# Sliding-window attention: dense key blocks on TensorE in place of shifted products on VectorE

## The chip, the core and the metric

The kernel runs on one core of a Trainium2 chip. The core has a matrix engine (TensorE, PE in the profile, with its weight loads as PEld), a vector engine (VectorE, DVE), an engine for pointwise functions (ScalarE, ACT), GpSimd (POOL) and a sync engine whose queue (SPq) issues transfers. PE reads its operands from SBUF and writes to PSUM, eight banks of 512 fp32 columns on 128 partitions. The metric is the device time of one execution in microseconds (us); lower is better.

## The reference

Four layers on a sequence of 2048 rows of 512 features, in the order A, B, A, B. Each adds to `x` a function of its layer norm. A is a long convolution whose kernel comes from a state-space model, done by Fourier transforms. B is what changes here:

```python
H = 32; Dh = D // H                     # 32 heads of 16 features
W, dil = 8, 2
qkv = (x @ wqkv) ...                    # (3, H, S, Dh)
idx = pos[:, None] - (jnp.arange(W) * dil)[None, :]
mask = idx >= 0
logits = jnp.einsum("bhsd,bhswd->bhsw", q, kg) * Dh ** -0.5
logits = jnp.where(mask, logits, -1e9)
attn = softmax(logits, axis=-1)
o = jnp.einsum("bhsw,bhswd->bhsd", attn, vg)
return o @ wo
```

So a query at position s looks at eight keys: s, s-2, s-4, to s-14. Even positions see only even ones, and odd ones only odd ones.

## The kernel before

The sequence stands in SBUF as `X[p, j, :]`, position 16 p + j, with 128 partitions p and 16 slots j. `kernel_and_first_conv` computes the convolution's kernel and the first A layer (0 to 268 us), `b_layer` the first attention layer (268 to 402), `a_layer` the second A layer (402 to 468), and `b_layer` again the second attention layer (468 to 602), with the store of the result.

An attention layer goes like this. `start(q)` norms four slots on DVE, transposes them on PE into `pt_x` and copies them to `xnT`, half of them by ACT (L807) and half by DVE (L805), so that features stand on partitions and positions in columns, ordered j first. `proj_qk` (L815) makes queries and keys with four matmuls of 512 columns a tile, copied out by ACT (L824). For each of the eight offsets w, `qk_products` (L845) multiplies queries with shifted keys on DVE (L855, and L863 where the shift crosses a partition), and PE sums groups of 16 features with the small matrix `bones` into `Lp` (L868). The logits are transposed back (L876), and `softmax` (L880) takes maximum, exponential (ACT, L902), sum, reciprocal and product on whole tiles. `proj_v` (L828) makes the values, and two transfers put a copy `Vp`, one partition lower, beside `V`. `pv` (L916) multiplies values with weights on DVE for each offset (L924), and PE adds the eight products by matmuls with the identity, which transpose them as well (L939); ACT copies the sum to `oT` (L942). `out` (L944) multiplies by `wo`, adds `X` by an identity matmul (L950) and copies back to `X` (L951). In the first attention layer it also gathers the statistics of the next norm.

`load_b_weights` (L116) loads the weights over SP's queue, with a permutation of `wo` in the transfer and one of the value weights on ACT (L831). `Conv.final` (L295) and `final` in `a_layer` (L744) write the convolution's result back to `X`, eight or four neighbouring slots at a time. `s1` in `a_layer` (L685) does the first stage of the transform, four slots at a time. `a_layer` holds four spectra `Kt` of 1 MB, loaded from DRAM.

The order within an engine comes from the framework's planner: it places instructions by priority, which is the order of the program, as soon as their inputs and a free buffer are there by its own costs. `at(tc, marks[q])` gives a part the priority of an earlier place in the program; `room` reserves such a place. Semaphores are added by the framework. Engines take their instructions in the order planned.

## Time and profile before

| | us |
|---|---|
| median of three runs | 604.02 |
| lowest and highest run | 603.73, 607.95 |
| span of the profiled execution | 606.0 |
| its two attention layers | 134, 134 |

The span is from the first to the last instruction of one profiled execution; the runs are device times of other executions, and the median stands 2.0 us under the span. The page gives busy time by engine, the span in 40 slices, the chain of work that ended last and the costliest groups of instructions. A row of a group reads: line, engine, operation, written tile <- read tiles, partitions x elements, count | busy us, mean ns of one | idle time just before them and what ended it. A row in order of time reads: start, us from start to end of the run of instructions, engine, line, operation, count. A matmul's duration contains its latency; in a run, the next one starts long before it is over.

### The profile page before, as it was taken

What the parts mean: (1) busy time and instruction counts of PE and PEld (TensorE: products, weight loads), DVE (VectorE), ACT (ScalarE), POOL (GpSimd) and SP (SyncE); (2) the same over time, 40 slices, a digit from 0 to 9 for tenths busy, and PEclk for the clock granted to TensorE, in tenths of its full rate; (3) what the DMA queues carried; (4) which work ended last, traced back from release to release, by engine and by line L of the source; (5) the groups of instructions that cost most, each with busy time, mean ns of one, the idle gap of its engine ahead of it and who ended that gap; (6) DMA issues with size and microseconds to landing.
All of it is one profiled execution on the core that took longest, in us unless ns stands there. A gap on an engine that the chain in (4) does not pass through costs nothing.

```text
span 606.0 us, 12631 instructions
## 1 busy us (share of the span) xinstructions
PE 422.6 (70%) x5362; PEld 261.7 (43%) x5402; DVE 497.0 (82%) x942; ACT 323.0 (53%) x449; POOL 12.9 (2%) x50
## 2 busy tenths in 40 slices
PE   1102565865775575559998678977996899857996
PEld 0101343562462463245333466644764433326762
DVE  5999999799899996366877899965999688689950
ACT  4999355455465343526576213466984556722144
POOL 0000000000000002100000000000000000000000
PEclk9999787696797797758999599997998899978999
DMA  8101354624735627510001333005530000040011
GB/s 293 62 1 35 61 104 66 140 55 106 121 98 99 103 91 136 129 70 1 1 1 39 83 137 143 2 1 125 85 71 0 2 1 1 1 121 1 1 71 69
DMA packets 75093, 41.31 MB, mean 68 GB/s; under 512 B 65825, under 2 KB 70818, under 8 KB 73758
## 3 DMA queue, kind: packets, MB, share of 16 engines
q1 hardware_dynamic: 73454, 40.12, 27.2%
q8 instruction: 42, 0.69, 0.5%
q10 hardware_dynamic: 1584, 0.39, 0.3%
q14 instruction: 13, 0.11, 0.1%
HBM read 15.89 MB, written 8.39 MB: 40 GB/s over the span
## 4 chain that ended last, share of the span: by engine, by line
PE 27%; DVE 21%; ACT 9%; issue 7%; DMA 2%; POOL 0%; SPq 0%; POOLq 0%; ACTq 0%
PE ps_qk L822 7%; DVE prod L924 6%; PE ps_o L948 4%; PE ps_v L836 3%; PE Lp L868 2%; PE pt_x L802 2%; PE po L939 2%; DVE prod L863 1%; DVE ln_st_b L152 1%; ACT xc L711 1%; DVE pa L719 1%; DMA zt<-Z 1%; DVE pb L720 1%; ACT oT L942 1%; PE ps_o L950 1%
## 5 line engine op out<-in xcount | busy, mean ns | idle before, releaser
L939 PE MATMUL po<-sb_ident,prod 128*128 128x128 bf16 x1024 | 70.4, 227 | 13.7 <-DVE prod L924 10.3
L939 PEld LDWEIGHTS <-prod 128*128 128x128 bf16 x1024 | 62.3, 102 | 23.5 <-DVE prod L924 20.1
L822 PE MATMUL ps_qk<-xnT,wqk 128*128 128x512 bf16 x245 | 63.7, 391 | 4.3 <-ACT xnT L807 2.3
L855 DVE TENSOR_TENSOR prod<-qT,kT 128x2048 bf16<-128x2048 bf16 (+3 forms) x48 | 43.2, 953 | 14.0 <-ACT qT L824 7.2
L924 DVE TENSOR_TENSOR prod<-V,L 128x2048 bf16<-128x2048 bf16 (+3 forms) x48 | 43.8, 955 | 6.4 <-PE po L939 6.4
L942 ACT CAST oT<-po 128x1024 bf16<-128x1024 f32 x16 | 15.4, 1015 | 56.6 <-PE po L939 56.6
L863 DVE TENSOR_TENSOR prod<-qT,kT 128x2048 bf16<-128x2048 bf16 (+3 forms) x40 | 35.0, 903 | 6.9 <-ACT kT L824 4.3
L204 PE MATMUL psA<-X,sb_F 128*128 128x128 bf16 x128 | 13.7, 237 | 34.5 <-ACT X L575 33.7
L822 PEld LDWEIGHTS <-wqk 128*128 128x128 bf16 x256 | 23.4, 100 | 32.1 <-issue 11.8
L948 PE MATMUL ps_o<-wo_t,oT 128*128 128x512 bf16 x121 | 33.5, 380 | 4.9 <-ACT oT L942 3.9
L204 PEld LDWEIGHTS <-sb_F 128*128 128x128 bf16 x256 | 17.4, 106 | 42.6 <-issue 40.0
L924 DVE TENSOR_TENSOR prod<-Vp,L 128x2048 bf16<-128x2048 bf16 (+3 forms) x40 | 35.0, 903 | 0.0
L532 PE MATMUL psk<-Ytab,Xtab 128*32 128x64 bf16 x1024 | 23.7, 206 | 12.9 <-DVE Ytab L513 5.6
L191 ACT CAST Z<-psA 128x1024 bf16<-128x1024 f32 (+1 forms) x32 | 28.6, 979 | 7.3 <-PE psA L204 7.3
L535 PE MATMUL psk<-Y2tab,Xtab 128*32 128x48 bf16 x1024 | 22.8, 202 | 13.5 <-issue 12.2
L868 PE MATMUL Lp<-prod,sb_bones 128*32 128x512 bf16 x256 | 24.9, 410 | 10.1 <-DVE prod L863 5.1
L513 DVE TENSOR_TENSOR Ytab<-Ytab,MA 128x2048 bf16<-128x2048 bf16 (+1 forms) x33 | 30.7, 931 | 0.2
L152 DVE BATCH_NORM_STATS2 ln_st_b<-X 128x6 f32<-128x384 bf16 (+2 forms) x80 | 23.7, 358 | 8.6 <-ACT X L309 8.6
L515 DVE TENSOR_TENSOR Y2tab<-Ytab,MB 128x2048 bf16<-128x2048 bf16 (+1 forms) x33 | 30.7, 930 | 0.0
L836 PE MATMUL ps_v<-wv,xnT 128*128 128x512 bf16 x126 | 28.2, 379 | 1.8 <-ACT V L838 1.7
L532 PEld LDWEIGHTS <-Xtab 128*32 128x32 bf16 x1024 | 20.9, 105 | 17.8 <-issue 15.5
L222 PE MATMUL psA<-zt,sb_C 128*128 128x512 bf16 x30 | 15.6, 548 | 18.6 <-DMA zt<-Z 14.4
(184 smaller groups left out, 1022.3 us busy)
## 6 DMA issues: line engine op xcount, KB each, us to landing
kt_scratch<-Kt SPq DMA_DIRECT2D x4, 1024.0 KB, 3.9
Kt<-kt_scratch SPq DMA_DIRECT2D x4, 1024.0 KB, 6.8
Vp<-V SPq DMA_DIRECT2D x2, 1568.0 KB, 9.1
X<-in_A_u_dram SPq DMA_DIRECT2D x4, 512.0 KB, 5.1
Xr<-in_A_u_dram SPq DMA_DIRECT2D x4, 512.0 KB, 5.1
out_dram<-X SPq DMA_DIRECT2D x4, 512.0 KB, 2.6
k_scratch<-KTq SPq DMA_DIRECT2D x7, 256.0 KB, 2.0
KT<-k_scratch SPq DMA_DIRECT2D x7, 256.0 KB, 2.8
```

The costliest lines, as they stand in the source:

```text
L204: nc.tensor.matmul(o, F1[:, j, r, :], rhs_j(j), start=True, stop=not dk)
L513: nc.vector.tensor_tensor(v(Y[:, :, :, q * EYB:(q + 1) * EYB, :]), src, vm(self.mult(self.MA, lev, hc, EYB)), ALU.mult)
L515: nc.vector.tensor_tensor(v(Y2[:, :, :, (q - 1) * EYB:q * EYB, :]), src, vm(self.mult(self.MB, lev, hc, EYB)), ALU.mult)
L532: nc.tensor.matmul(psk[32 * g:32 * g + 32, ds, :], xs, Y[:, m // 2, h, :, t], start=(m == 0), stop=False, skip_group_check=True)
L822: nc.tensor.matmul(ps[:], wqk[:, ct, f0:f0 + 128], xnT[:, ct, s0:s0 + 512], start=(ct == 0), stop=(ct == 3))
L836: nc.tensor.matmul(ps[:].rearrange("p a b -> p (a b)"), xnT[:, ct, j * 128:(j + 1) * 128], wv[:, ct, :], start=(ct == 0), stop=(ct == 3))
L855: nc.vector.tensor_tensor(pr[:, :, (ja - j0) * 128:(ja - j0) * 128 + n], qT[fp][:, :, ja * 128: ja * 128 + n], kT[fp][:, :, (ja - sh) * 12 ...
L863: nc.vector.tensor_tensor(pr[:, :, 0:n], qT[fp][:, :, q0: q0 + n], kT[fp][:, :, k0: k0 + n], ALU.mult)
L868: nc.tensor.matmul(Lp[r0:r0 + 32, w // 4, :], bones[:, w % 4, :], pr[:, f2, hb * 512:(hb + 1) * 512], start=(w % 4 == 0), stop=(w % 4 == 3 ...
L924: nc.vector.tensor_tensor(p2[:, ja - j0: ja - j0 + n, :].rearrange("p j (t d h) -> p (j t) d h", t=2, d=DH), src.rearrange("p j (t d h) -> ...
L939: nc.tensor.matmul(po[f2][:, jj, :], p2[:, jj, f2 * 128:(f2 + 1) * 128], ident[:], start=(w == 0 and jj % 4 == 0), stop=(w == W - 1), skip ...
L948: nc.tensor.matmul(ps[:], oT[:, ft, j * 128:(j + 1) * 128], wo_t[:, ft, :], start=(ft == 0), stop=False)
```

## The change

The eight shifted products are replaced by dense matmuls. Positions are split by parity, and each parity's 1024 positions into 9 blocks of 114 queries, which need the 7 keys before the first one: 121 keys, held in a block of 128. For each of 4 quarters `n` (parity by half of the heads) and 9 blocks `b`, `logits` multiplies a head's keys by its queries, 128 by 114, as 16 matmuls for 16 heads. A head has 16 features, but its matmul contracts over 32 rows: the other 16 hold constants (`_mask_rows`), whose product adds a large negative number wherever the key lies outside the window of eight. Two heads share 32 partitions, one in the even and one in the odd rows; `KS` and `QS` hold both arrangements, and the constants are loaded once. ACT takes the exponential straight from PSUM, without subtracting a maximum. `values` uses the exponentials as the stationary operand and a head's 16 values, with a column of ones, as the moving one of 17 columns: the last column is the sum. DVE takes its reciprocal and scales; PE transposes the result back, two matmuls a block, and DVE copies three blocks at a time to `oT`.

Queries and keys reach `KS` and `QS` by transfers, because the features have to be spread over every second partition: ACT and DVE copy a projection to `st`, and SP issues two transfers for each pair of projections, 32 of 128 KB a layer. The quarter `n + 1` is projected during quarter `n`, in two sets of buffers. The 8 output projections of the even positions are placed in the last quarter, the others behind it.

So that four slots of one parity can go together, slots are taken in the order given by `slot` in the norms' statistics, in `final`, in `s1`, and in the store. The copies in `Conv.final` are now of four slots each. `a_layer` keeps two spectra `Kt` at a time. The weights and the constants are loaded over GpSimd's queue, and ACT permutes the query and key weights once. The diff, cut to its core:

```diff
+def slot(m):
+
+    g, i = m // 4, m % 4
+    return 8 * (g % 2) + 2 * i + g // 2
...
-def load_b_weights(nc, const, C, wqkv, wo):
...
+def load_b_weights(nc, const, tmp, C, wqkv, wo):
     wqk = const.tile([128, 4, 1024], BF, name="wqk")
     wv = const.tile([128, 4, 512], BF, name="wv")
     wo_t = const.tile([128, 4, 512], BF, name="wo_t")
-    wvn = const.tile([128, 4, 512], BF, name="wvn")
     wsrc = wqkv.rearrange("(t p) f -> p t f", p=128)
-    nc.sync.dma_start(wqk[:], wsrc[:, :, 0:1024])
-    nc.sync.dma_start(wvn[:], wsrc[:, :, 1024:1536])
-    for ft in range(4):
-        src = wo[ft * 128:(ft + 1) * 128, :].rearrange("(h d) o -> d h o", d=DH)
-        nc.sync.dma_start(wo_t[:, ft, :], src)
-    nc.sync.dma_start(C["bones"][:], nc.inline_tensor(_bf(bones_np), name="c_bones").ap())
-    Vp = const.tile([128, 2, NJ - 2, 256], BF, name="Vp")
-    nc.gpsimd.memset(Vp[0:1], 0.0)
-    return dict(wqk=wqk, wv=wv, wvn=wvn, wo=wo_t), Vp
+    eng = nc.gpsimd
+    wq_in = tmp.tile([128, 4, 1024], BF, name="wq_in")
+    eng.dma_start(wq_in[:], wsrc[:, :, 0:1024])
+    for w in range(2):
+        for e in range(2):
+            nc.scalar.copy(wqk[:, :, w * 512:w * 512 + 512].rearrange("p t (g d e) -> p e t g d", d=DH, e=2)[:, e],
+                           wq_in[:, :, w * 512:w * 512 + 512].rearrange("p t (g e d) -> p e t g d", d=DH, e=2)[:, e])
+    mask = nc.inline_tensor(_bf(_mask_rows()), name="c_mask").ap()
+    sets = []
+    for u in range(2):
+        sets.append([const.tile([128, 2, 2, UW], BF, name=f"{nm}{u}") for nm in ("KS", "QS")])
+        for w, T in enumerate(sets[u]):
+            nc.gpsimd.memset(T[:, :, :, 0:UF], 0.0)
+            nc.gpsimd.memset(T[:, :, :, UF + 1024:UW], 0.0)
+            for e in range(2):
+                eng.dma_start(T[1 - e::2, e], mask[w].unsqueeze(1).to_broadcast([64, 2, UW]))
+        if u == 0:
+            eng.dma_start(wv[:], wsrc[:, :, 1024:1536])
+            eng.dma_start(wo_t[:], wo.rearrange("(t p) o -> p t o", p=128))
+    return dict(wqk=wqk, wv=wv, wo=wo_t, sets=sets)
...
-            self.nc.vector.bn_stats(self.st[:, j, part, :], X[:, j, a:b])
+            self.nc.vector.bn_stats(self.st[:, j, part, :], X[:, slot(j), a:b])
...
-            nc.scalar.copy(X[:, jh * nj:(jh + 1) * nj, dc * DCH + x0:dc * DCH + x1],
-                           ps[:].rearrange("p q j d -> p (q j) d")[:, :, 0:n])
+                nc.tensor.matmul(ps[:, q, :, 0:n], self.C["ident"][:], slots(Xr[:], m)[:, :, x0:x1], start=False,
+                                 stop=True, skip_group_check=True)
+            for q in range(nq):
+                nc.scalar.copy(slots(X[:], jh * nq + q)[:, :, dc * DCH + x0:dc * DCH + x1], ps[:, q, :, 0:n])
...
-        kp = es.enter_context(tc.tile_pool(name="a_kt", bufs=4))
+        kp = es.enter_context(tc.tile_pool(name="a_kt", bufs=2))
...
+                j = slot(q * 4 + jj)
-            nc.scalar.copy(Z[dc][:, :, :, q * 32:(q + 1) * 32], ps[:])
+            dst = Z[dc][:].rearrange("k r i (g j t d) -> k g t (r i) j d", g=2, t=2, d=8)[:, q % 2, q // 2]
+            nc.scalar.copy(dst, ps[:].rearrange("k r i (j d) -> k (r i) j d", d=8))
...
+def b_layer(nc, tc, C, X, Wt, ln_b, marks, store=None, ln_next=None):
+        big = es.enter_context(tc.tile_pool(name="b_big", bufs=1))
+        xnp = es.enter_context(tc.tile_pool(name="b_xn", bufs=8))
+        stp = es.enter_context(tc.tile_pool(name="b_st", bufs=4))
+        sm = es.enter_context(tc.tile_pool(name="b_sm", bufs=3))
+        psS = es.enter_context(tc.tile_pool(name="b_psS", bufs=2, space=PSUM))
+        psG = es.enter_context(tc.tile_pool(name="b_psG", bufs=4, space=PSUM))
+        ident = C["ident"]
+        wqk, wv, wo_t, sets = Wt["wqk"], Wt["wv"], Wt["wo"], Wt["sets"]
+        xnT = big.tile([128, 4, 2, UP], BF, name="xnT")
+        oT = big.tile([128, 4, 2, QW], BF, name="oT")
+        V = big.tile([128, 2 * NB, H, DH + 1], BF, name="V")
+        PT = [big.tile([128, 16 * NQ + 16], BF, name=f"PT{k}") for k in range(3)]
...
+        def start(g):
+            par, j0 = g // 2, (g % 2) * 4
+            xn = []
+            for i in range(4):
+                xn.append(xnp.tile([128, D], BF, name="xn", tag="xn"))
+                ln_b.norm(xn[i][:], X[:, slot(g * 4 + i), :], g * 4 + i)
+            for ch in range(2):
+                pt = gps([128, 4, 2, 128], BF)
+                for i in range(4):
+                    for c in range(2):
+                        ct = ch * 2 + c
+                        nc.tensor.transpose(pt[:, i, c, :], xn[i][:, ct * 128:(ct + 1) * 128], ident[:])
+                for c in range(2):
+                    dst = xnT[:, ch * 2 + c, par, UF:UF + 1024].rearrange("c (p j) -> c p j", j=8)[:, :, j0:j0 + 4]
+                    (nc.vector.tensor_copy if ch == 0 else nc.scalar.copy)(
+                        dst, pt[:, :, c, :].rearrange("c j p -> c p j"))
+        st = {}
+        def proj(n, k):
+            par, fp = n // 2, n % 2
+            f2, which, h = k // 4, k // 2 % 2, k % 2
+            if h == 0:
+                st[n] = stp.tile([128, 1024], BF, name="st", tag="st")
+            f0 = which * 512 + (fp * 2 + f2) * 128
+            ps = gps([128, 512])
+            for ct in range(4):
+                nc.tensor.matmul(ps[:], wqk[:, ct, f0:f0 + 128], xnT[:, ct, par, UF + h * 512:UF + h * 512 + 512],
+                                 start=(ct == 0), stop=(ct == 3))
+            (nc.scalar.copy if h else nc.vector.tensor_copy)(st[n][:, h * 512:h * 512 + 512], ps[:])
+            if h:
+                T = sets[n % 2][1 - which]
+                for e in range(2):
+                    nc.sync.dma_start(T[e::2, e, f2, UF:UF + 1024], st[n][e::2, :])
+        def vproj(par, b):
+            ps = gps([128, H, DH])
+            for ct in range(4):
+                nc.tensor.matmul(ps[:].rearrange("p h d -> p (h d)"), xnT[:, ct, par, NQ * b + 1:NQ * b + 1 + NK],
+                                 wv[:, ct, :], start=(ct == 0), stop=(ct == 3))
+            nc.vector.tensor_copy(V[:, par * NB + b, :, 0:DH], ps[:])
+        def logits(n, b):
+            KS, QS = sets[n % 2]
+            pt = PT[(n * NB + b) % 3]
+            for ih in range(2):
+                S4 = psS.tile([128, 2, 512], F32, name="S4", tag="S4")
+                for sl in range(4):
+                    f2, e = sl // 2, sl % 2
+                    for ii in range(2):
+                        r = slice(32 * (ih * 2 + ii), 32 * (ih * 2 + ii) + 32)
+                        nc.tensor.matmul(S4[:, ii, sl * NQ:(sl + 1) * NQ], KS[r, e, f2, b * NQ + 1:b * NQ + 1 + NK],
+                                         QS[r, e, f2, UF + b * NQ:UF + b * NQ + NQ],
+                                         start=True, stop=True, skip_group_check=True)
+                nc.scalar.activation(pt[:, ih * 8 * NQ:(ih + 1) * 8 * NQ].rearrange("k (i x) -> k i x", i=2),
+                                     S4[:, :, 0:4 * NQ], ACT.Exp, scale=DH ** -0.5)
+        pts = {}
+        def values(n, b):
+            par, fp = n // 2, n % 2
+            pt = PT[(n * NB + b) % 3]
+            O = gps([128, 16, DH + 1])
+            for i in range(4):
+                for sl in range(4):
+                    f2, e = sl // 2, sl % 2
+                    c0 = (i * 4 + sl) * NQ
+                    nc.tensor.matmul(O[:, f2 * 8 + i * 2 + e, :], pt[:, c0:c0 + 128],
+                                     V[:, par * NB + b, (fp * 2 + f2) * 8 + i * 2 + e, :], start=True, stop=True,
+                                     skip_group_check=True)
+            rd = sm.tile([128, 16], F32, name="rd", tag="rd")
+            nc.vector.reciprocal(rd[0:NQ], O[0:NQ, :, DH])
+            on = sm.tile([128, 256], BF, name="on", tag="on")
+            nc.vector.tensor_tensor(on[0:NQ].rearrange("q (h d) -> q h d", d=DH), O[0:NQ, :, 0:DH],
+                                    rd[0:NQ].unsqueeze(2).to_broadcast([NQ, 16, DH]), ALU.mult)
+            return on
+        ons = {}
+        def turn_o(n, b):
+            par, fp = n // 2, n % 2
+            if b % 3 == 0:
+                pts[n] = gps([128, 3, 2, NQ], BF)
+            on = ons.pop((n, b))
+                nc.tensor.transpose(pts[n][:, b % 3, f2, :], on[0:NQ, f2 * 128:(f2 + 1) * 128], ident[0:NQ, 0:NQ])
+            if b % 3 == 2:
+                dst = oT[:, fp * 2:fp * 2 + 2, par, (b - 2) * NQ:(b + 1) * NQ].rearrange("f t (b q) -> f t b q", q=NQ)
+                nc.vector.tensor_copy(dst, pts[n][:].rearrange("f b t q -> f t b q"))
+        def out(m):
+            j = slot(m)
+            par, jp = j % 2, j // 2
+            ps = gps([128, 512])
+            for ft in range(4):
+                nc.tensor.matmul(ps[:], oT[:, ft, par, 0:1024].rearrange("f (p j) -> f j p", j=8)[:, jp],
+                                 wo_t[:, ft, :], start=(ft == 0), stop=False)
+            nc.tensor.matmul(ps[:], ident[:], X[:, j, :], start=False, stop=True)
+            nc.scalar.copy(X[:, j, :], ps[:])
+            if m % 4 == 3:
+                if store is not None:
+                    store(m // 4)
+                if ln_next is not None:
+                    ln_next.gather(X, 0, m - 3, m + 1)
+                    ln_next.finish(m - 3, m + 1)
+                    out_marks.append(room(tc, 8))
+        for g in range(2):
+            with at(tc, marks[g]):
+                start(g)
+        for k in range(8):
+            proj(0, k)
+        for g in range(2, 4):
+            with at(tc, marks[g]):
+                start(g)
+        todo = []
+        LA, LT = 2, 4
+        for t in range(4 * NB + LT):
+            if t < 4 * NB:
+                n, b = t // NB, t % NB
+                logits(n, b)
+                if n % 2 == 0:
+                    vproj(n // 2, b)
+                if n < 3 and b < 8:
+                    proj(n + 1, b)
+                if n == 3 and b < 8:
+                    out(b)
+            if t >= LA and t - LA < 4 * NB:
+                n, b = (t - LA) // NB, (t - LA) % NB
+                ons[n, b] = values(n, b)
+            if t >= LT:
+                turn_o((t - LT) // NB, (t - LT) % NB)
+        for m in range(8, 16):
+            out(m)
...
-            store=lambda j0, j1: nc.sync.dma_start(ov[:, j0:j1, :], X[:, j0:j1, :]))
+    b_layer(nc, tc, C, X, Wt, ln_b2, marks,
+            store=lambda m: nc.sync.dma_start(slots(ov, m), slots(X[:], m)))
```

268 lines of the change are left out of this document (63 added, 205 removed).

## The prediction

> **What bounds the kernel now.** I read the page first (busy shares and the chain of work that ended last), then the table of stages, then the groups of instructions by line, and last the order of time inside the attention layers, for the pace of one engine.
>
> ```profile
> span 606.0 us, 12631 instructions
> PE 422.6 (70%) x5362; PEld 261.7 (43%) x5402; DVE 497.0 (82%) x942; ACT 323.0 (53%) x449; POOL 12.9 (2%) x50
> PE 27%; DVE 21%; ACT 9%; issue 7%; DMA 2%; POOL 0%; SPq 0%; POOLq 0%; ACTq 0%
> ...
> 268.00:402.00 134.00, 116.84 (x998) 67.33 (x1009) 113.12 (x197) 63.18 (x94) 2.21 (x14) 0.92 0.13 46
> 402.00:468.00 66.00, 51.75 (x457) 36.05 (x463) 54.26 (x121) 48.47 (x67) 0.00 (x0) 0.92 0.32 64
> 468.00:602.00 134.00, 114.34 (x998) 65.52 (x1008) 99.35 (x158) 61.52 (x90) 2.21 (x14) 0.95 0.08 26
> ```
>
> The last three rows are stages: their length, then busy time of PE, PEld, DVE, ACT, POOL, then clock and DMA. The two attention layers take 134 us each. In both, PE and DVE are busy nearly all the time and ACT under half of it, and the chain goes back and forth between PE and DVE. No single engine is the bound: each waits for the other.
>
> ```profile
> L924 DVE TENSOR_TENSOR prod<-V,L 128x2048 bf16<-128x2048 bf16 (+3 forms) x48 | 43.8, 955 | 6.4 <-PE po L939 6.4
> L855 DVE TENSOR_TENSOR prod<-qT,kT 128x2048 bf16<-128x2048 bf16 (+3 forms) x48 | 43.2, 953 | 14.0 <-ACT qT L824 7.2 <-PE Lp L868 6.8
> L924 DVE TENSOR_TENSOR prod<-Vp,L 128x2048 bf16<-128x2048 bf16 (+3 forms) x40 | 35.0, 903 | 0.0
> L863 DVE TENSOR_TENSOR prod<-qT,kT 128x2048 bf16<-128x2048 bf16 (+3 forms) x40 | 35.0, 903 | 6.9 <-ACT kT L824 4.3 <-PE Lp L868 2.6
> L939 PE MATMUL po<-sb_ident,prod 128*128 128x128 bf16 x1024 | 70.4, 227 | 13.7 <-DVE prod L924 10.3 <-ACT oT L942 1.3
> ```
>
> The products on DVE are 43.8 + 43.2 + 35.0 + 35.0 = 157 us, 78.5 a layer. All of them go. What comes instead lies mostly on PE and ACT, so the question is how long PE needs for a layer.
>
> **PE's paces.** A matmul's listed duration holds its latency; the pace is the distance of starts in a run.
>
> ```profile
> 582.99 1.03 PE L948 MATMUL ps_o<-wo_t,oT 128*128 128x512 bf16 x4
> 583.85 0.38 PE L950 MATMUL ps_o<-X,sb_ident 128*128 128x512 bf16 x1
> 584.07 1.03 PE L948 MATMUL ps_o<-wo_t,oT 128*128 128x512 bf16 x4
> ...
> 585.15 6.70 PE L939 MATMUL po<-sb_ident,prod 128*128 128x128 bf16 x117
> ...
> 239.97 0.56 PE L323 MATMUL psu<-KTu,sb_F 128*128 128x32 bf16 x16 [0.94 <-ACT Z L327]
> ...
> 233.12 0.50 PEld L323 LDWEIGHTS <-sb_F 128*128 128x128 bf16 x16
> ...
> L939 PEld LDWEIGHTS <-prod 128*128 128x128 bf16 x1024 | 62.3, 102 | 23.5 <-DVE prod L924 20.1 <-issue 1.0
> ...
> 295.48 1.04 PE L822 MATMUL ps_qk<-xnT,wqk 128*128 128x512 bf16 x4
> 296.44 0.40 PE L868 MATMUL Lp<-prod,sb_bones 128*32 128x512 bf16 x4
> 296.78 1.04 PE L822 MATMUL ps_qk<-xnT,wqk 128*128 128x512 bf16 x4
> ```
>
> From 582.99 to 584.07 are five matmuls of 512 columns: 0.216 us each. 117 of 128 columns in 6.70 us: (6.70 - 0.22) / 116 = 0.056 us. Sixteen of 32 columns, each with a fresh 128x128 weight load: (0.56 - 0.18) / 15 = 0.025 us; their loads come as fast, (0.50 - 0.10) / 15 = 0.027. The last three rows give the price of changing the array's tiling: four full matmuls and four in 32-column tiles, which run side by side (four in 0.40 us, where one of 512 columns lasts 0.38), repeat every 1.30 us; without the change it would be 4 x 0.216 + 0.22 = 1.08, so two changes cost 0.21, one 0.105.
>
> **The change, PE, for one layer.** Unchanged: q/k projections 32 x 4 x 0.216 = 27.6; output projections 16 x 1.08 = 17.3; transposes of xn 64 x 0.056 = 3.6. Value projections become 18 groups instead of 16: 18 x 0.864 = 15.6. Gone: 512 po matmuls (28.7), 128 Lp in fours (32 x 0.22 = 7.0) with their tiling changes, 32 transposes (1.8). New, for 36 blocks of 114 queries:
> - Values, 16 a block, full weight load and 17 columns. Ends: 0.025 (the L323 run) and 0.102 (a load that nothing hides, the PEld row). L323 has the same load and nearly the same column count, so 0.026: 576 x 0.026 = 15.0.
> - Logits, 16 a block, 32 contraction rows, 114 columns, two row groups taking turns into two banks. The trace has no row groups. One after the other they cost 114/512 x 0.216 = 0.048; two at a time 0.024, as the 32-column tiles do it. I take 0.030, nearer to those tiles: 17.3. The far end is 0.048 + 0.105 = 0.153, if each turn costs as much as a change of tiling. The Trainium skill, "TensorE: Matmul & The Clock Gate", Part 3, says that matmuls in differing row groups run at the same time; by it this term would be an estimated 13.8, and no run here shows it yet.
> - Tiling changes: two a block if both halves of the logits stand together, four if the planner puts other work between; three at 0.105: 11.3.
> - Transposes of the result: 72 x 0.056 = 4.0.
>
> Sum 27.6 + 17.3 + 3.6 + 15.6 + 15.0 + 17.3 + 11.3 + 4.0 = 111.7 us, where the same paces give the old layer 99.8 plus some 6 of tiling changes. So PE gets more work, not less; the gain can only be in the waiting, now 134 - 106 = 28 us a layer.
>
> A rule that speaks against the change: the Trainium skill, same page, "LDWEIGHTS (loading the stationary operand)", gives a load as columns / 1.2 ns, 107 ns for 128; by it the values alone would be an estimated 61 us a layer. The L323 rows disagree, with a load every 27 ns.
>
> **ACT, DVE and the queues.**
>
> ```profile
> L942 ACT CAST oT<-po 128x1024 bf16<-128x1024 f32 x16 | 15.4, 1015 | 56.6 <-PE po L939 56.6
> L902 ACT ACTIVATE L<-L 128x2048 bf16<-128x2048 bf16 x4 | 7.6, 1910 | 7.8 <-DVE L L900 7.7
> L951 ACT CAST X<-ps_o 128x512 bf16<-128x512 f32 x32 | 18.2, 586 | 15.2 <-PE ps_o L950 15.2
> L902 ACT ACT_TABLE_LOAD x2 | 2.6, 1283 | 0.6 <-DVE L L900 0.6
> L831 ACT COPY wv<-wvn 128x512 bf16<-128x512 bf16 x4 | 4.3, 1118 | 1.9 <-DMA wvn<-in_B_wqkv_dram 1.9
> ...
> 406.50 2.84 ACT L695 CAST Z<-ps_s 128x1024 bf16<-128x1024 f32 x3 [0.16 <-PE ps_s L693]
> ...
> L742 DVE CAST VT<-vp 128x512 bf16<-128x512 f32 x16 | 11.0, 686 | 0.4 <-ACT VT L740 0.4
> L805 DVE COPY xnT<-pt_x 128x1024 bf16<-128x1024 bf16 x8 | 5.5, 688 | 2.6 <-PE pt_x L802 2.5
> L908 DVE TENSOR_TENSOR sm_den<-sm_s 128x256 f32<-128x256 bf16 x4 | 1.7, 420 | 0.0
> L159 DVE RECIPROCAL ln_rstd_b<-ln_den_b 128x4 f32<-128x4 bf16 x8 | 1.4, 173 | 1.6 <-ACT ln_den_b L158 1.5
> L911 DVE RECIPROCAL sm_rdb<-sm_den 128x256 bf16<-128x256 f32 x4 | 7.0, 1749 | 0.0
> ...
> 239.23 0.53 SPq L127 DMA_DIRECT2D wqk<-in_B_wqkv_dram  x1
> ...
> k_scratch<-KTq SPq DMA_DIRECT2D x7, 256.0 KB, 2.0
> wqk<-in_B_wqkv_dram SPq DMA_DIRECT2D x1, 1024.0 KB, 5.7
> Kt<-kt_scratch SPq DMA_DIRECT2D x4, 1024.0 KB, 6.8
> ...
> 267.90 1.31 DVE L163 TENSOR_SCALAR xn<-X,ln_rstd_b,ln_nb_b 128x512 bf16<-128x512 bf16 x4
> ...
> 271.34 0.59 PE L822 MATMUL ps_qk<-xnT,wqk 128*128 128x512 bf16 x1 [1.15 <-ACT xnT L807]
> ```
>
> ACT: an exponential of 912 elements alone is 1015 - 112 x 0.87 = 917 ns (0.87 = (1910 - 1015) / 1024); back to back three of 1024 took 2.84, so 0.91 is the pace and 0.82 that of 912. Between 0.82 and 0.92 I take 0.87: 72 x 0.87 = 62.6. With 16 q/k copies and 16 output copies at 0.586 (18.8) and 8 xnT copies (4.7) ACT has 86 us. In the first layer the last quarter mixes the root of the next norm with exponentials: up to four table loads, 5.1 more. ACT stays under PE's 112, but not by quarters: the second has PE 9 x 1.32 + 8 x 0.864 = 18.8 and ACT 9 x 1.74 + 4 x 0.586 = 18.0, the fourth PE 20.5 against ACT 20.3 to 25. There they wait for each other.
>
> DVE: reciprocal of 16 elements between L159 and L911, 173 + 12 x 6.25 = 248 ns; scaling 256 elements 420; 18 value copies and 16 q/k copies at 0.686; 12 copies of the result at about 0.5; 8 of xnT at 0.69; 16 norms at 0.4: 36 x 0.67 + 23.3 + 6 + 5.5 + 6.4 = 65. It no longer binds.
>
> Queues: SP gets 32 copies of 128 KB a layer, which land in some 2 to 3 us (KTq). Those of the next quarter are issued at least one block before use and lie under PE's other work; only the first quarter's are open, 1 to 4 us, since PE has value projections to do meanwhile. The Vp copies (with their waits on SP for V) go. The second attention store goes out in shorter runs, 0 to 2 us at the end. POOL's queue carries the weights and mask rows, 4.4 MB instead of 2.1; at the pace of wqk 25 us from 239 (where wqk is issued now) to 264, before the layer starts at 268. Behind the first of them ACT has four permuting copies of 1024 elements, 4 to 9 us by L831, against four of 1.1 that go: 0 to 5 us in a stretch where ACT has room; I take 1. The convolution layer keeps two Kt instead of four, so 2 MB arrive during it, 6.8 each, beside the transposing copies: 0 to 5, I take 1. Slot permutation, statistics, the copies of `final` (two of 512 for one of 1024): 0 to 2, ACT has room; I take 0.
>
> **The sum.** A layer: PE 111.7; opening to the first projection 3.4 (267.90 to 271.34, as now); first q/k copies 2; the end 4.5 (the last exponentials 1.8, values 0.4, reciprocal and scaling 0.7, transposes, copy 0.5, hand-overs, before eight output projections that are in PE's sum); waits between PE and ACT 2 (0 to 10). Together 123.6, 10.4 under 134. Both layers: 20.8. 606.0 - 20.8 + 1 + 1 + 1 (store) = 588.2 for a profiled execution. That one stood 2.0 above the median of 604.0, so 586.
>
> Bounds: logits 0.024, two tiling changes and no waits give 111.7 - 3.5 - 3.8 and 7 for opening and end: 111.4 a layer and 562. Logits one by one (+10.4), four changes (+3.8) and 10 of waits instead of 2 give 145.8 and 631.
>
> **Rivals.**
> 1. The waits stay (the other side). PE's work grows by 6 us a layer; if hand-overs between PE, ACT and DVE leave as much waiting as now, 28 us, a layer takes 140: 604 + 12 + 3 = 619. For it: four groups a block share four banks, one held over three blocks by the transposed results, and PE takes its work in order. Against it: values come two blocks and transposes four blocks after their logits, longer than any copy above. It decides once 22 of the 28 stay.
> 2. Logits one after another, 0.048 each: 10.4 more a layer uses the gain up, 586 + 21 = 607, no change. For it: nothing here shows row groups side by side; against it the four 32-column tiles.
> 3. Weight loads are not hidden behind 17 columns: 0.102 instead of 0.026, 44 a layer, 586 + 88 = 674. The L323 run speaks against it. This is what the page's load rule would do here.
> 4. All hand-overs hidden, tiling changed twice a block: 562 to 570.
>
> **Chances.** My own case, 570 to 597: 0.46. Rival 4: 0.16. Rival 2 or a mixture that ends within 1%: 0.18. Rival 1: 0.16. Rival 3 or a row-group turn that costs like a change of tiling: 0.04. About 1%, 6 us, is what a measurement of this kernel can tell from no change. So faster 0.62, same 0.18, slower 0.20. The range 558 to 622 leaves out some 0.05 below and 0.13 above; that of the likeliest alone is 570 to 597.
>
> **What would show it.** In the new profile: exponentials at 0.8 to 0.95 us and 72 a layer; values at 0.025 to 0.03 from start to start; logits in a run at 0.024 to 0.03 (right) or 0.048 (rival 2); DVE's busy time in the layers down to some 65 to 80; PE busy nearly all of a layer of about 124 us; waits of PE for ACT small. Wrong would be a layer over 130 with PE idle behind exponentials or copies (rival 1), values at 0.1 (rival 3), or first logits later than 17 us after the first norm, because masks or weights arrive late.

## The result and the profile after

The changed kernel takes 586.21 us (median of four runs, 584.88 to 587.44), the kernel before 605.90 in the four runs beside it: a ratio of 0.968, 95% interval 0.9635 to 0.9718. Times here go by fast runs; of all runs one was slow, 634.6 us of `e9_one_group`, and is left out. The forecast was 586. The profiled execution of the changed kernel spans 583.1 us. Its page, with the same rows as before (span, busy time by engine, chain by engine):

```profile
span 583.1 us, 15269 instructions
PE 421.7 (72%) x6522; PEld 262.6 (45%) x6522; DVE 425.7 (73%) x966; ACT 374.8 (64%) x511; POOL 17.9 (3%) x56
PE 35%; DVE 9%; ACT 6%; DMA 5%; issue 3%; SPq 0%; ACTq 0%; DVEq 0%
```

The chain that went back and forth between PE and DVE is now mostly PE. By stage (length, busy PE, PEld, DVE, ACT, POOL, then clock and DMA), cut at the first norm and the last copy of `X` of each attention layer:

```profile
0.00:272.80 272.80, 144.45 (x2922) 94.47 (x2922) 230.42 (x468) 151.49 (x207) 14.76 (x48) 0.82 0.44 107
272.80:393.20 120.40, 113.07 (x1568) 65.69 (x1569) 75.07 (x203) 90.02 (x122) 0.00 (x0) 0.96 0.10 37
393.20:463.00 69.80, 54.68 (x464) 37.47 (x464) 57.21 (x133) 48.05 (x66) 3.01 (x8) 0.90 0.50 121
463.00:579.20 116.20, 109.53 (x1568) 64.96 (x1568) 63.02 (x167) 85.22 (x116) 0.15 (x2) 0.97 0.15 52
```

| stage | before, same cuts | after | forecast | measured |
|---|---|---|---|---|
| first part | 267.9 | 272.8 | +1 | +4.9 |
| attention 1 | 134.7 | 120.4 | -10.4 | -14.3 |
| convolution layer | 65.8 | 69.8 | +1 | +4.0 |
| attention 2 | 133.6 | 116.2 | -10.4 | -17.4 |
| store | 4.1 | 3.9 | +1 | -0.2 |

So the sum came out by two errors of opposite sign: the attention layers gained 10.9 us more than forecast, the rest lost 5.7 more. Against its own profile the forecast of 588.2 was 5 us too long. That the median fits better is chance: I took 2 us off for the median of the first three runs before, and the profiled execution after stands 3 us under its median. In the same way the stages add up to 22.9 us between the two profiled executions, where the medians differ by 19.7: some 3 us of the stages' differences belong to the executions that were profiled.

The groups by line (busy, mean ns of one, idle before) give the prices of the new operations:

```profile
L911 ACT ACTIVATE PT<-S 128x912 bf16<-128x912 f32 x144 | 126.1, 938 | 31.5 <-PE S L908 31.2
L928 DVE RECIPROCAL rd<-psG 114x16 f32<-114x16 f32 x72 | 18.3, 254 | 41.8 <-PE psG L924 41.8
L908 PE MATMUL S<-QS,KS 32*128 32x114 bf16 x1152 | 43.1, 211 | 5.9 <-DMA KS<-st 4.1 <-ACT PT L911 1.0
L924 PE MATMUL psG<-V,PT 128*128 128x17 bf16 x1152 | 40.9, 171 | 0.9 <-ACT PT L911 0.6 <-DVE on L930 0.2
L930 DVE TENSOR_TENSOR on<-psG,rd 114x256 bf16<-114x256 f32 x72 | 30.1, 419 | 1.6
```

PE waits 5.9 us for the logits' inputs and 0.9 for the values', over both layers (a wait inside a run of matmuls is not in these figures). Reciprocal and scaling take 254 and 419 ns where the forecast has 248 and 420; they are DVE's, and DVE is off the path. The order of time on PE shows the paces, first in the first quarter, then in the steady part of it:

```profile
291.55 0.23 PE L908 MATMUL S<-QS,KS 32*128 32x114 bf16 x4 [1.06 <-DMA KS<-st]
291.71 0.61 PE L895 MATMUL psG<-wv,xnT 128*128 128x512 bf16 x2
...
300.08 0.37 PE L908 MATMUL S<-QS,KS 32*128 32x114 bf16 x8
300.39 1.04 PE L895 MATMUL psG<-wv,xnT 128*128 128x512 bf16 x4
...
305.21 0.55 PE L924 MATMUL psG<-V,PT 128*128 128x17 bf16 x16
305.62 0.26 PE L942 MATMUL psG<-sb_ident,on 114*128 114x114 bf16 x2
305.81 0.40 PE L908 MATMUL S<-QS,KS 32*128 32x114 bf16 x16
306.14 1.04 PE L895 MATMUL psG<-wv,xnT 128*128 128x512 bf16 x4
307.02 1.03 PE L884 MATMUL psG<-xnT,wqk 128*128 128x512 bf16 x4
307.88 0.56 PE L924 MATMUL psG<-V,PT 128*128 128x17 bf16 x16
```

Sixteen values: (0.55 - 0.17) / 15 = 0.025 us each, as forecast. The logits are the surprise. From the start of a run of them to the start of what follows, 4 take 0.16 us, 8 take 0.31 and 16 take 0.33: the second eight are nearly free. The forecast for 16, with its three changes of tiling, was 0.48 + 0.32 = 0.80.

In the second and fourth quarters ACT has stretches with hardly a gap. Its order of time there:

```profile
320.48 1.75 ACT L911 ACTIVATE PT<-S 128x912 bf16<-128x912 f32 x2 [0.17 <-PE S L908]
322.12 0.59 ACT L886 CAST st<-psG 128x512 bf16<-128x512 f32 x1
322.62 1.75 ACT L911 ACTIVATE PT<-S 128x912 bf16<-128x912 f32 x2
324.54 1.75 ACT L911 ACTIVATE PT<-S 128x912 bf16<-128x912 f32 x2 [0.17 <-PE S L908]
...
551.90 1.79 ACT L911 ACTIVATE PT<-S 128x912 bf16<-128x912 f32 x2
553.53 0.63 ACT L955 CAST X<-psG 128x512 bf16<-128x512 f32 x1
554.00 1.83 ACT L911 ACTIVATE PT<-S 128x912 bf16<-128x912 f32 x2
555.63 0.67 ACT L955 CAST X<-psG 128x512 bf16<-128x512 f32 x1
```

Exponentials and copies follow one another with at most 0.17 us between them; two blocks take 4.06 us (320.48 to 324.54) where PE's work for them is some 3.6. On PE the runs of logits of the second quarter last longer for it:

```profile
328.13 0.73 PE L908 MATMUL S<-QS,KS 32*128 32x114 bf16 x16
328.79 1.04 PE L884 MATMUL psG<-xnT,wqk 128*128 128x512 bf16 x4
...
330.27 0.52 PE L908 MATMUL S<-QS,KS 32*128 32x114 bf16 x16
330.72 0.56 PE L924 MATMUL psG<-V,PT 128*128 128x17 bf16 x16
```

From start to start these two runs of 16 take 0.66 and 0.45 us; all runs of 16 in the first and third quarters take 0.33 or 0.34. The difference is read as PE standing inside the run until ACT has emptied a bank of `S`.

### The profile page after: what moved, and what is told of

Read it like the earlier page. It is cut to its first block, busy times and chain, and to the rows that moved or that the text cites. A ratio compares the mean times of both kernels' runs of the same rounds, so it can differ in the third digit from the quotient of the medians.

```text
span 583.1 us, 15269 instructions
## 1 busy us (share of the span) xinstructions
PE 421.7 (72%) x6522; PEld 262.6 (45%) x6522; DVE 425.7 (73%) x966; ACT 374.8 (64%) x511; POOL 17.9 (3%) x56
## 4 chain that ended last, share of the span: by engine, by line
PE 35%; DVE 9%; ACT 6%; DMA 5%; issue 3%; SPq 0%; ACTq 0%; DVEq 0%
PE psG L884 9%; PE S L908 5%; PE psG L952 5%; PE psG L895 5%; PE psG L924 3%; ACT PT L911 3%; DMA KS<-st 2%; DMA zt<-Z 2%; DVE ln_st_b L202 2%; PE psG L867 1%; PE ps_s L745 1%; PE psG L954 1%; DVE pa L772 1%; PE psG L942 1%; DVE pb L773 1%
## 5 line engine op out<-in xcount | busy, mean ns | idle before, releaser
L911 ACT ACTIVATE PT<-S 128x912 bf16<-128x912 f32 x144 | 126.1, 938 | 31.5 <-PE S L908 31.2
L884 PE MATMUL psG<-xnT,wqk 128*128 128x512 bf16 x256 | 67.4, 385 | 1.1 <-DVE xnT L870 1.1
L908 PE MATMUL S<-QS,KS 32*128 32x114 bf16 x1152 | 43.1, 211 | 5.9 <-DMA KS<-st 4.1
L924 PEld LDWEIGHTS <-PT 128*128 128x128 bf16 x1152 | 39.0, 96 | 16.6 <-ACT PT L911 1.3
L897 DVE CAST V<-psG 128x512 bf16<-128x512 f32 x36 | 25.0, 694 | 23.2 <-PE psG L895 23.2
L924 PE MATMUL psG<-V,PT 128*128 128x17 bf16 x1152 | 40.9, 171 | 0.9 <-ACT PT L911 0.6
L908 PEld LDWEIGHTS <-KS 32*128 32x128 bf16 x1152 | 25.8, 93 | 29.2 <-issue 15.6
L895 PE MATMUL psG<-wv,xnT 128*128 128x512 bf16 x144 | 38.7, 382 | 0.0
L952 PE MATMUL psG<-wo_t,oT 128*128 128x512 bf16 x128 | 38.4, 410 | 0.3 <-DVE oT L945 0.2
L254 PEld LDWEIGHTS <-sb_F 128*128 128x128 bf16 x256 | 18.1, 111 | 43.1 <-issue 40.9
L272 PE MATMUL psA<-zt,sb_C 128*128 128x512 bf16 x30 | 15.4, 546 | 27.7 <-DMA zt<-Z 23.4
L886 DVE CAST st<-psG 128x512 bf16<-128x512 f32 x32 | 22.0, 687 | 15.4 <-PE psG L884 14.1
L930 DVE TENSOR_TENSOR on<-psG,rd 114x256 bf16<-114x256 f32 x72 | 30.1, 419 | 1.6
L241 ACT CAST xc<-psA 128x1024 bf16<-128x1024 f32 x16 | 15.8, 1014 | 22.1 <-PE psA L275 22.1
```

Of the source, the lines that this page charges most:

```text
L241: self.nc.scalar.copy(dst, src)
L254: nc.tensor.matmul(o, F1[:, j, r, :], rhs_j(j), start=True, stop=not dk)
L884: nc.tensor.matmul(ps[:], wqk[:, ct, f0:f0 + 128], xnT[:, ct, par, UF + h * 512:UF + h * 512 + 512], start=(ct == 0), stop=(ct == 3))
L895: nc.tensor.matmul(ps[:].rearrange("p h d -> p (h d)"), xnT[:, ct, par, NQ * b + 1:NQ * b + 1 + NK], wv[:, ct, :], start=(ct == 0), stop=( ...
L897: nc.vector.tensor_copy(V[:, par * NB + b, :, 0:DH], ps[:])
L908: nc.tensor.matmul(S4[:, ii, sl * NQ:(sl + 1) * NQ], KS[r, e, f2, b * NQ + 1:b * NQ + 1 + NK], QS[r, e, f2, UF + b * NQ:UF + b * NQ + NQ], ...
```

## The experiments

All stage lengths below are cut as in the table. Between kernels that leave a stage as it is, the first part varied from 272.4 to 276.6 us, the second attention layer from 115.6 to 117.8 and the convolution layer from 69.3 to 70.0; less than this isn't read as an effect. The kernel before ran beside each of them, with medians of 605.75 to 607.52, so kernels are compared by their ratios to it. Where the interval of a ratio overlaps that of the changed kernel (0.9635 to 0.9718), the total does not tell the two apart, and the argument rests on the stages alone.

**The first part: 4.9 us.** In the changed kernel POOL issues the load of `wq_in` early, because nothing stands before it on that queue:

```profile
230.02 0.88 POOL L168 DMA_DIRECT2D wq_in<-in_B_wqkv_dram  x1 [45.92 <-PE psA L254]
```

SP's queue then:

```profile
231.54 6.75 SPq L219 DMA_TRANSPOSE zt<-Z  x2
238.40 1.07 SPq L701 DMA_DIRECT2D KTu<-k_scratch  x2
...
246.19 6.87 SPq L219 DMA_TRANSPOSE zt<-Z  x4
```

Before, SP's queue had this:

```profile
228.53 0.38 SPq L649 DMA_DIRECT2D KTu<-k_scratch  x1
229.55 3.59 SPq L169 DMA_TRANSPOSE zt<-Z  x2
233.19 0.58 SPq L649 DMA_DIRECT2D KTu<-k_scratch  x1
```

Run `e1_late_wq` holds the load back with a small copy from the last spectrum:

```diff
                 cv.block(2 + u, xc, Kt, VT)
+        C["gate"] = ln.den[0:2, 0:2]
+        nc.gpsimd.tensor_copy(C["gate"], Kt[0:2, 3, 0, 0:2])
...
+    nc.gpsimd.tensor_copy(wq_in[0:2, 0, 0:2], C["gate"])
     eng.dma_start(wq_in[:], wsrc[:, :, 0:1024])
```

> Only the load of wq_in is moved: it is issued after the last spectrum of the first part (some 25 us later) instead of at 230.0. Theory (the load collides with the transposing copies of the first part): the two copies at 231.5 take about 3.6 us again instead of 6.75, KTu is loaded some 3 us earlier, the first part ends at 269 to 270 instead of 272.8, and the whole is 3 us shorter, about 583. Rival A (the order of SP's queue, where the KTu loads now stand behind the transposing copies, costs the time): the copies get shorter but the end of the first part moves by under 1 us, 585 to 587. Rival B (ACT's four permuting copies, 5.2 us together, cost the time): they now stand nearer to the end of the first part, which ends no earlier or up to 3 us later, 586 to 589.

Measured: 584.17 us, ratio 0.9635 (0.9587 to 0.9683). SP's queue and, below, PE in the opening of the attention layer:

```profile
230.73 2.65 SPq L220 DMA_TRANSPOSE zt<-Z  x2
233.48 1.11 SPq L702 DMA_DIRECT2D KTu<-k_scratch  x2
```

```profile
270.53 1.37 PE L870 MATMUL psG<-sb_ident,xn 128*128 128x128 bf16 x16 [0.34 <-DVE xn L214]
277.44 8.45 PE L887 MATMUL psG<-xnT,wqk 128*128 128x512 bf16 x29 [5.54 <-ACT xnT L873]
```

The two transposing copies take 2.65 us instead of 6.75, and the first norm comes at 268.4, 4.4 us earlier: the collision is shown, and the changed order on SP is not what costs. (The four copies behind them still take 6.44, beside the mask rows.) But rival B's work takes the gain: `wq_in` lands at 269, ACT does its permuting copies in front of `xnT`, PE waits 5.54 us, and the first logits start at 288.3, where they started at 287.9.

`e1c_late_all` adds the same hold (`nc.gpsimd.tensor_copy(T[0:2, :, 0, UF], C["gate"])`) to the four tiles of mask rows.

> The load of wq_in and the mask rows are all issued after the last spectrum of the first part. Theory (collision): as with wq_in alone, and the four transposing copies at 246.2, which took 6.87 us beside the mask loads, take about 5 (two pairs of 2.5 before), so the first part ends at 268 to 269 and the whole is 4 to 5 us shorter, about 582. Rival A (the masks did no harm): the same as with wq_in alone. Rival B (the masks now arrive too late): the first logits stand more than 17 us after the first norm, instead of 15.1, and what the first part gains is lost there, 585 to 588.

Measured: 585.34 us, 0.9666 (0.9605 to 0.9728). The four later copies go from 6.87 to 5.89 us, but the first norm is only at 271.3, and the first logits at 289.9. ACT's order of time says why:

```profile
267.39 1.32 ACT L172 COPY wqk<-wq_in 128x1024 bf16<-128x1024 bf16 x1 [4.08 <-DMA wq_in<-in_B_wqkv_dram]
268.58 0.91 ACT L364 CAST X<-psA 128x256 bf16<-128x256 f32 x3
```

The first permuting copy stands before the last copies of `X` in ACT's queue, and waits 4.08 us for `wq_in`. Rival B in its result, but not by the masks' arrival.

`e1d_after_turn` holds the load of `wq_in` and the masks until the last transposing copies are done (the small copy reads `zt` of the last `spectrum32` instead of `Kt`).

> The load of wq_in, and the mask rows behind it, are issued right after the last transposing copies of the first part (about 247), instead of at 230 before the first ones, or at 260.8 as in the first run of this study. What the first run showed: the copies took 2.65 us instead of 6.75 and the first norm came 4.4 us earlier, but wq_in landed at 269, ACT's permuting copies stood between the norm and the transposes of xn, and the first logits came at 288.3, as late as with no change. Theory (both ends have to be met): wq_in lands at about 256, ACT copies it by 263 in a stretch where it waits for PE, the first norm is at 268 to 269.5, the first logits some 15 us later at 283.5 to 285, and the whole is 3 to 4.5 us shorter, 582 to 583.5. Rival (the masks, now after wq_in, or the store of Kt delay the first copies into KS): first norm at 268 to 269.5 but first logits at 287 or later, 585 to 587.

Measured: first norm 269.4, first logits 285.2, 2.7 us earlier than with no change; 585.39 us, 0.9652 (0.9595 to 0.9708). By the stages the theory holds in the main, somewhat smaller than expected; by total time this run can't be told from the changed kernel.

**The convolution layer: 4.0 us.** All its norms start only when the attention layer is over:

```profile
392.72 3.95 DVE L213 TENSOR_SCALAR U<-X,ln_rstd_a,ln_nb_a 128x512 bf16<-128x512 bf16 x12
```

`e2_own_u` allocates `U` before the first attention layer:

```diff
-        U = big.tile([128, NJ, D], BF, name="U")
...
+    U = const2.tile([128, NJ, D], BF, name="U")
     marks = b_layer(nc, tc, C, X, Wt, ln_b, marks, ln_next=ln)
```

> U of the convolution layer gets memory of its own, allocated before the first attention layer. Theory (the 4.7 us lost in that stage come from U standing in memory that the attention layer holds until its end, so that all 16 norms start at 392.7): the norms of the first two quarters start before the attention layer ends, as in the kernel before, and the stage takes 66 to 67.5 us instead of 71.0; the whole 581.5 to 583. Rival A (the Kt loads, two of them during the stage, delay the transposing copies): the norms start earlier but the stage stays at 70 to 71, 585 to 587. Rival B (norms inside the attention layer take DVE from its values): the stage gets shorter but the attention layer longer by as much, 585 to 587.

```profile
374.83 1.38 DVE L213 TENSOR_SCALAR U<-X,ln_rstd_a,ln_nb_a 128x512 bf16<-128x512 bf16 x4
...
387.43 1.38 DVE L213 TENSOR_SCALAR U<-X,ln_rstd_a,ln_nb_a 128x512 bf16<-128x512 bf16 x4
```

Measured: the stage takes 65.7 us, as before the change, with `Kt` still in two buffers: the cause is `U`'s memory. The first attention layer became 2.0 us longer (122.4), though, and the total is 584.06, 0.962 (0.9557 to 0.9684). Rival B names the norms inside that layer for it, but the extra lies before them: from the first norm to the first logits the layer takes 18.5 us instead of 15.1, and from there to its end 103.9 instead of 105.2. The last two runs show a cause, a memset beside the first norms.

**The logits.** `e9_one_group` takes the side-by-side work away:

```diff
-                        r = slice(32 * (ih * 2 + ii), 32 * (ih * 2 + ii) + 32)
+                        r = slice(0, 32)
```

> All sixteen logits of a block use the 32 contraction rows of the first row group (the other heads' logits are left out; the number and size of the instructions are the same). In the changed kernel a run of 8 logits (two row groups) holds PE for 0.32 us and one of 16 (four row groups) for 0.33. Theory (matmuls of different row groups run side by side, whatever their order, those of one row group one behind the other at 0.048 us): a run of 8 takes 0.19 us more and one of 16 takes 0.58 us more; with 36 runs of 8 and 47 of 16 that is 34 us of PE, of which some 6 to 10 lie beside ACT's work: 608 to 618. Rival (a logits matmul costs 0.013 to 0.024 us whatever its row group, and a run costs 0.3 for entering and leaving): 584 to 590.

```profile
302.81 0.57 PE L908 MATMUL S<-QS,KS 32*128 32x114 bf16 x8
303.31 0.39 PE L895 MATMUL psG<-wv,xnT 128*128 128x512 bf16 x1
```

Measured: 619.67 us, 1.0202 (1.0148 to 1.0256), a little over the theory's range. In a run, starts are (0.57 - 0.21) / 7 = 0.051 apart instead of (0.37 - 0.21) / 7 = 0.023, and eight logits take 0.50 us instead of 0.31, the 0.19 expected. Its runs of 4, 8, 12 and 16 take 0.30, 0.50, 0.70 and 0.90 us: 0.05 for a matmul, and 0.10 beside them for both changes of tiling. The attention layers take 137.6 and 131.7 us, 17.2 and 15.5 more, together close to the 34 of the theory. So row groups do run side by side, two in a run of 8 and four in one of 16.

`e3_serial` leaves the row groups and only changes the order, `for ii` outside `for sl` instead of inside.

> The logits of a half block are issued four and four of the same row group, instead of two row groups taking turns; nothing else is changed. Theory (two row groups run side by side only when neighbours in PE's order differ in row group; that is where the pace of 0.021 us comes from): the pace becomes about 0.048 (114 columns at 0.216 us per 512), 0.027 x 16 x 72 = 31 us more of PE, of which a quarter lies beside ACT's work in the second and fourth quarters: the attention layers 10 to 15 us longer each, 606 to 616. Rival A (the pace does not depend on the order): 0.021 stays, 585 to 588. Rival B (a fourth of the neighbours still differ and the array looks ahead): 0.028 to 0.035, 594 to 602.

Measured: 590.70 us, 0.9726 (0.9675 to 0.9778). My theory falls: runs of 8 and 16 take 0.32 and 0.34 us as before, so neighbours in PE's order need not differ in row group. The total is 3 us over rival A's range, but the intervals overlap. In the profiled execution the second attention layer takes 121.7, 5.5 more. Of that, 3.5 lie in its third quarter: 28.6 us instead of 25.1, with a mean granted clock of 0.88 there instead of 1.00. The rest, with 107 runs of logits instead of 103, stays open.

`e4_split` issues the second half's logits behind the block's projections.

```diff
-                logits(n, b)
+                logits(n, b, 0)
...
+            if t < 4 * NB:
+                logits(t // NB, t % NB, 1)
             if t >= LA and t - LA < 4 * NB:
```

> Each block's value projection and q/k or output projection are put between the two halves of its logits. In PE's order of instructions the two attention layers then have 316 changes between logits and full matmuls instead of 206. Theory (a change costs 0.105 us, as read in the prediction): 110 x 0.105 = 11.6 us more, of which up to 3 lie beside ACT's work in the second quarter: 594 to 598. Rival A (a change costs nothing that PE's pace shows): 584 to 588. Rival B (the two exponentials of a block no longer run one behind the other, and the values two blocks later wait for the second): over 600, with PE waiting for PT at the values.

Measured: 602.23 us, 0.9914 (0.9880 to 0.9947); the attention layers 129.3 and 124.6, 17.3 us more together in the profiled executions (some 14 by the two ratios). PE's wait for `PT` at the values is 1.6 us instead of 0.6, so rival B has its total but not its cause. The price by change was too low, and it is the wrong measure. Counted in PE's order, the changed kernel has 47 runs of 16 logits, 4 of 12, 36 of 8 and 16 of 4; at 0.33, 0.33, 0.315 and 0.165 us that is 30.8. This one has 132 of 8, 6 of 6, 10 of 4 and 10 of 2; at 0.315, some 0.24, 0.165 and some 0.12, 45.9. The difference, 15.1, is most of what the layers lost: a run of 8 in two row groups costs as much as one of 16 in four.

**The boundaries of quarters.** `e6_early`:

```diff
-                if n < 3 and b < 8:
-                    proj(n + 1, b)
+                if n < 3 and b < 7:
+                    for k in ((0, 1) if b == 0 else (b + 1,)):
+                        proj(n + 1, k)
```

> The eight q/k projections of the next quarter are issued in seven blocks instead of eight (two in the first), so that the last copies into KS and QS are issued one block earlier. Theory (at each boundary of quarters PE waits for the last copy into KS, 2 to 4 us on the chain): the waits at the six boundaries after an opening go, 3 to 6 us together, 580 to 583. Rival (the copies are covered by values and transposes of the two blocks before, or another wait, for the banks of psG, takes their place): 585 to 588.

Measured: 585.38 us, 0.9655 (0.9591 to 0.9719). The total lies in the rival's range. The profiled execution, the fastest of the four, spans 579.0, with attention layers of 118.1 and 114.0, 2.3 and 2.2 shorter. PE's wait for `KS` falls only from 4.1 to 3.1 us. Of the rest, 2.4 us fit the logits: 57 runs of 16 instead of 47, 91 runs in all, 28.4 us at the prices above instead of 30.8. So the waits that the theory names gave 1 us, and the other 3.5 of the layers came mostly by another way.

`e6b_early2` issues two projections in each of the first four blocks.

> The eight q/k projections of the next quarter are issued in the first four blocks, two each. Theory (the wait for the copies at the boundaries costs 3 to 6 us): it goes altogether, as with the milder version, 579 to 583. Rival (PE has too much in the first four blocks and too little in the last five, where ACT then sets the pace at 1.75 us a block): the last blocks of a quarter take 1.8 to 1.9 us, the first ones 3.4, and since PE idles behind ACT the layers get longer, 588 to 596.

Measured: 591.72 us, 0.9746 (0.9693 to 0.9798), layers of 121.7 and 118.1. The total lies in the rival's range, and its picture is there: in the last blocks of the second quarter seven exponentials stand back to back in 6.18 us (from 520.01), 1.77 a block. But its price isn't shown, because the granted clock fell in the same places: 0.50 from 523 to 532 and 0.59 from 330 to 340, where single matmuls of 512 columns last 0.59 us instead of 0.38. At the full clock the 9 us from 523 would hold some 4.5 us of matmuls, more than the 1.3 and 1.9 us that the layers lost. Whether the fall of the clock comes from PE's idling was not tested.

**The roots.** `e7_root` puts `ln_next.finish` for the first two quarters behind the last logits in the program.

> The roots of the next norm's statistics for the first two quarters are issued after the last logits of the first attention layer instead of between exponentials. Theory (three table loads of 1.28 us stand between exponentials in the last quarter, and ACT is near its limit there): two of them go in effect, and the first attention layer (119.2 us, where the second one takes 116.2) becomes 1.5 to 2.5 us shorter; the whole 583.5 to 585. Rival (PE sets the pace of that quarter and the table loads lie beside its work): under 0.7 us, 585.5 to 586.5.

Measured: 587.36 us, 0.9692 (0.9631 to 0.9752). The run says nothing about the theory: the planner placed the roots between the exponentials all the same, and the three table loads of 1.28 us stand at 369.8, 371.5 and 380.9, as before at 370.3, 372.4 and 381.9.

**Together.** `f1_together` is `e1d_after_turn`, `e2_own_u` and `e6_early` in one.

> Three changes that worked on their own stage, put together: wq_in and masks loaded after the last transposing copies, U with memory of its own, and the projections of the next quarter one block earlier. Theory (the stages add up): the first part 3 to 4.5 us shorter, the convolution layer 4 to 5 (65.7 instead of 70.3 when alone), the attention layers 2 each: 586 - 4 - 4.5 - 4 = 572 to 576. Rival (U's norms inside the first attention layer lengthen it by the 2.5 us seen when alone, and the earlier first norm is given back before the first logits): 578 to 582.

Measured: 577.30 us, 0.9529 (0.9492 to 0.9565): faster than the changed kernel, whose interval begins at 0.9635. First norm 269.1, convolution layer 65.7, but a first attention layer of 123.3. Its first norms, and what POOL did:

```profile
269.12 3.33 DVE L215 TENSOR_SCALAR xn<-X,ln_rstd_b,ln_nb_b 128x512 bf16<-128x512 bf16 x4
```

```profile
268.65 2.52 POOL L850 MEMSET V<- 128x576 bf16 x1
```

`e2_own_u` has the same 3.33 us at 272.9, 2.0 of its longer opening. In the changed kernel, where the memset of `V` came earlier, the same two rows were these:

```profile
272.82 1.31 DVE L213 TENSOR_SCALAR xn<-X,ln_rstd_b,ln_nb_b 128x512 bf16<-128x512 bf16 x4
```

```profile
264.51 2.55 POOL L847 MEMSET V<- 128x576 bf16 x1
```

`f2_dve_memset` adds two edits to it: `nc.vector.memset(V[:, :, :, DH], 1.0)` instead of `nc.gpsimd`, and the hold of `wq_in` for `wv` and `wo` too. (In the text below, the ones of the changed kernel were set from 264.5 to 267.1 us.)

> As the three changes together, and two more: the ones of V are set by DVE instead of POOL, and wv and wo are loaded behind wq_in. In the run with the three changes the first four norms took 3.33 us instead of 1.31, while POOL's 2.5 us of setting ones (267 us earlier in the changed kernel, where the memory of V came free before the norms) ran beside them. Theory (the two engines hinder each other): the first four norms take 1.3 to 1.4 us again, the first logits come 15 to 17 us after the first norm instead of 19.0, and the whole is 2 us shorter than 577.3, 574 to 576. Rival (the norms are slow for another reason, the place of xn in memory): 3.33 stays, 577 to 578.

```profile
266.48 1.34 DVE L217 TENSOR_SCALAR xn<-X,ln_rstd_b,ln_nb_b 128x512 bf16<-128x512 bf16 x4
...
277.92 0.54 DVE L852 MEMSET V<- 128x576 bf16 x1 [1.92 <-issue]
```

Measured: 574.35 us, 0.9472 (0.9420 to 0.9523), the lowest ratio here, though its interval overlaps that of `f1_together`. The norms are back at 1.34, so the place of `xn` is not the cause, and the first attention layer takes 120.1. First logits come 17.7 us after the first norm, a little more than expected. The convolution layer takes 65.8 and the second attention layer 115.2, as in `f1_together` (65.7 and 115.5). The first norm comes 2.6 us earlier; the run has two edits more, and which of them did that isn't separated.

## Why the prediction came out as it did

- **Right.** DVE has left the path, and most of the gain is waiting that went: PE's listed wait for the logits' inputs and the values is under 7 us for both layers. Exponentials run at 0.875 (0.87 forecast), values at 0.025 (0.026), so weight loads are hidden (rival 3 is out). The Trainium skill, "TensorE: Matmul & The Clock Gate", "LDWEIGHTS (loading the stationary operand)", gives columns / 1.2 ns, 107 ns for such a load. The trace lists these loads at 96 ns each, but here one and its matmul follow the last pair after 25, so the figure is near the length of a load and not its price. The Trainium skill, same page, Part 3, says that matmuls in differing row groups run at the same time; `e9_one_group` agrees, with 0.31 us for eight logits against 0.50.
- **The logits and the changes of tiling were mis-sized:** 17.3 + 11.3 = 28.6 us a layer forecast, 30.8 / 2 = 15.4 measured. I took two row groups at a time and each change as a separate 0.105. Four run at a time when 16 stand together; of a run of 16, 4 x 0.048 = 0.19 is work and some 0.14 pays for both changes (0.10 in `e9_one_group`). With 15.4 the PE sum of a layer is 98.5, and 101 with what values and transposes take more (below), under the 106 of before: PE did not get more work, as the prediction has it, but less. The trace of before had no row groups, and the rule that does have them was weighed and then set aside for a value between.
- **Not all of that reached the time.** Of these 13.2 us a layer, 7.4 arrived in the second one (116.2 against 123.6), and 5.8 did not. Some of that is PE's own: values and transposes of a block take 0.60 us (305.21 to 305.81) instead of 0.53, 2.6 a layer. The rest must be waits, for which the sum had 2. In the second quarter the forecast had PE at 18.8 and ACT at 18.0. Measured, ACT needs 9 x 1.75 + 4 x 0.59 = 18.1, and PE's logits there 3.4 us instead of a quarter of 28.6, which leaves PE 15.1, or 15.8 with its share of the 2.6. From its first logits to those of the third quarter it takes 18.75 us in both layers, so next to nothing of PE's saving arrives. The first and third quarters take 25.1 each in the second layer, where the forecast's prices give PE 26.6: 1.5 from each. The other 4.4 lie in the fourth quarter, the end and the waits, and were not taken apart. That ACT holds the second quarter is worked out from the rows; no run took ACT's work away.
- **The first attention layer is 4.2 us longer than the second**, and all of it lies behind the first logits of the fourth quarter (37.3 us to the end of the layer, 31.3 in the second one; the parts ahead of that are 1.9 shorter together). Three table loads of 1.28 us stand there, and the granted clock is lower as well: 0.55 from 357.8 to 361 and 0.76 from 380 to 387, against 1.00 for that part of the second layer. No run separates the two.
- **The first part, forecast +1, measured +4.9.** The step that failed is the one on queues: I let the loads begin at 239, where SP had issued them, and asked only whether they were done by 268. On POOL's queue nothing stood before the load of `wq_in`: it started when its memory was free, at 230, and ran beside the transposing copies. And the cost of the permuting copies is where they stand in ACT's queue, as `e1_late_wq` shows, not their 5 us.
- **The convolution layer, forecast +1 for `Kt`, measured +4.0.** I looked for a transfer and missed a release: bigger pools in `b_layer` reach into the memory that `U` takes, so its norms can't start before the pools are closed (all of them stand behind 392.7). `e2_own_u` gives all of it back in this stage.
- **Rivals.** Rival 2 would have been dearer than I priced it: `e9_one_group`, all in one row group, costs some 33 us over the changed kernel (619.7 against 586.2), not 21. Rival 1 is out in its form, waits between PE, ACT and DVE; a part of its kind, ACT in the second quarter, is there. Rival 4's 111.4 us a layer was not reached.

## What to carry to other kernels

When work moves to another queue or its tiles grow, ask when its memory is free and what runs at that moment, not only when its result is needed: a load that starts too early, and a pool that is released too late, cost 4 to 5 us each here. When PE's part of a stage gets cheaper, work out the other engines' sums for each stretch of the loop before counting the gain. Small matmuls that run side by side should be issued in the longest runs that the buffers allow: here 8 in two row groups cost as much as 16 in four. Before a difference of a few us between two profiled executions is given a cause, compare the granted clock of the stretch in which it lies.
